# A new instruction order for agent attention with an expert stage: loads batch by batch, TensorE's changes of kind priced by pair

## The chip, the core and the metric

One core of a Trainium2 chip runs the whole program in one launch. The core has five instruction streams, each of which runs in its own order: TensorE (PE in the tables, with its weight loads as PEld), VectorE (DVE), ScalarE (ACT), GpSimd (POOL) and SyncE (SP), which here issues nearly all of the transfers between device memory and the on-chip buffers. The metric is the device time of one execution in microseconds; the median over several executions counts.

## The reference

Four batches of 12608 tokens of 128 channels pass through two softmax products over 49 agents; then 128 tokens of each batch, those with the highest gate score, pass through an expert of two layers.

```python
def sm(a, b):
    s = scale * (a @ b.transpose(0, 2, 1))
    s = s - s.max(-1, keepdims=True)
    e = np.exp(s)
    return e / (e.sum(-1, keepdims=True) + 1e-09)
agent_v = sm(agents, k) @ v
x = sm(q, agents) @ agent_v
# expert stage, batch by batch
top_idx = np.argpartition(-scores[b], capacity)[:capacity]   # scores = x @ w_gate, capacity = 128
h = np.maximum(x[b, top_idx] @ w1, 0.0)
out[b, top_idx] = x[b, top_idx] + sigmoid(scores) * (h @ w2)
```

## The kernel before

**Tiling.** A batch is cut into seven chunks: six of 15 columns of 128 tokens and one of 9. For each batch and chunk there is a load of transposed keys (`xT_b_c` from `kT`), of values (`v_b_c`, one more column of ones) and of transposed queries (`xT_b_c` from `qT`); a large one is 960 KB (0.98 MB), a small one 0.59 MB. All of them, and the output tiles `og` of three batches, share one ring of six buffers (`inp`, N_IN = 6).

**Stages of a batch `b`.** `k`: TensorE makes the scores of a chunk in two halves (`S`, four matmuls side by side in 32-column tiles each), VectorE transposes each half into `sk` and takes its maximum (`mx`). `kmax`: two small products (`mT`, `mB`) make the maximum per agent of all seven chunks and spread it over the partitions (`mb`). `exp`: GpSimd subtracts it from `sk`, ScalarE takes the exponential. `av`: TensorE multiplies `sk` with `v`. `fin`: two small products (`pw`, `pp`) normalise and scale the result into `ws`. `q`: scores of the queries into `sq` (as for keys, with `qm` as maximum). `qe`: GpSimd subtracts, ScalarE takes the exponential; the value is split into two f16 halves in `f` by ScalarE and GpSimd (batch 0 also divides by its sum here). `turn`: TensorE transposes `f` (`fT`), ScalarE or VectorE copies it to `ft`. `gate`: a three-column product per token column gives the gate score (`pg`). `rank`: the 128 best tokens are found (`all`, `gt`, `pc`). `fill` (batch 0) and `out` (the others): TensorE forms the output (`po`), two engines scale it into `og`, SP stores it. `expert`: rows are gathered (`xq`), recomputed, put through the two layers (`ph`, `py`) and scattered (`out` from `ey`), batches 0, 1 and 2 as one group and batch 3 as another. The keys' `sk` tiles have a ring of nine buffers (N_SK = 9), so with seven chunks of one batch alive only two of the next batch find room until the first `av` of the older batch is done.

**What sets the order.** The body records every operation with what it depends on. `place` then runs a list scheduler over them: an operation that is ready is taken by its rank, a number in the table RANKS for its stage, batch, chunk and engine, less a bonus (STICK) if its kind is that of the last one on the engine; on TensorE a change of kind is charged in the planner's time (AFTER, line 253, used at line 352), and SLACK is added for what TensorE hands to others. Every engine's instructions are emitted in the order that comes out, and each engine then waits in that order. The constants are loaded at the top of `agent_attention_moe`: the agents (`ag_sb`), the table of constants (`cst`, 0.29 MB) and the gate weights (`wg_sb`) are issued from ScalarE's queue and their two ends of the expert's weights from SP's.

```python
key = rank[op.seq]
if op.kind == last[e]:
    key = (key[0] - stick, key[1])
...
if last[e] != op.kind:
    op.start += AFTER.get(last[e], 50.0)
```

Of the kernel before, what the change touches and what calls it, by code (L numbers as in the profile page):

```python
# [285 lines left out]
def place(rec, urgency, slack=0.0, stick=0.0):  # L286
# [89 lines left out]
    ('kmax', 0): {"DVE": -294641.053, "PE": -133586.107},  # L376
    ('exp', 0, 0): {"POOL": -143817.163, "ACT": -125982.646},
    ('exp', 0, 1): {"POOL": -963.973, "ACT": -99042.757},
    ('exp', 0, 2): {"POOL": -12481.222, "ACT": -37799.646},
    ('exp', 0, 3): {"POOL": -38853.391, "ACT": -33869.568},  # L380
    ('exp', 0, 4): {"POOL": 16185.168, "ACT": 11872.97},
    ('exp', 0, 5): {"POOL": 28821.359, "ACT": 10861.678},
    ('exp', 0, 6): {"POOL": 14920.899, "ACT": -98349.058},
    ('v', 0, 0): {"SP": -4348.542},
    ('av', 0, 0): {"PE": 5144.545},
    ('v', 0, 1): {"SP": -20520.697},
    ('av', 0, 1): {"PE": 41745.014},
    ('v', 0, 2): {"SP": -3630.195},
    ('av', 0, 2): {"PE": -28204.714},
    ('v', 0, 3): {"SP": -1826.223},  # L390
    ('av', 0, 3): {"PE": -44870.335},
    ('v', 0, 4): {"SP": -689.478},
    ('av', 0, 4): {"PE": -6385.343},
    ('v', 0, 5): {"SP": -461.295},
    ('av', 0, 5): {"PE": 47815.339},
    ('v', 0, 6): {"SP": -404.037},
    ('av', 0, 6): {"PE": 43409.94},
    ('fin', 0): {"DVE": -143642.174, "PE": -132722.281, "POOL": -39179.482, "ACT": -144313.857},
    ('q', 0, 0): {"SP": -704.547, "PE": 9683.405, "DVE": -297487.497},
    ('qe', 0, 0): {"POOL": 11484.086, "ACT": -127061.75, "DVE": -286160.382},  # L400
    ('turn', 0, 0): {"PE": -25559.309, "DVE": -3909.353, "ACT": -76846.925},
    ('gate', 0, 0): {"PE": 21754.42},
    ('q', 0, 1): {"SP": -11511.72, "PE": -165916.237, "DVE": -81122.367},
    ('qe', 0, 1): {"POOL": -9668.74, "ACT": 88899.289, "DVE": 62352.526},
    ('turn', 0, 1): {"PE": -33340.912, "DVE": -134369.208, "ACT": -37052.354},
    ('gate', 0, 1): {"PE": 19893.715},
    ('q', 0, 2): {"SP": -9823.687, "PE": -68234.899, "DVE": 12201.11},
    ('qe', 0, 2): {"POOL": 9370.151, "ACT": 15865.887, "DVE": -114474.214},
    ('turn', 0, 2): {"PE": 25264.138, "DVE": 6840.329, "ACT": -32474.095},
    ('gate', 0, 2): {"PE": 56157.267},  # L410
    ('q', 0, 3): {"SP": -351.313, "PE": 32070.707, "DVE": 29764.455},
    ('qe', 0, 3): {"POOL": 179974.323, "ACT": -58982.455, "DVE": -279699.82},
    ('turn', 0, 3): {"PE": -176895.194, "DVE": -411535.852, "ACT": -99983.463},
    ('gate', 0, 3): {"PE": 5350.803},
    ('q', 0, 4): {"SP": -771.424, "PE": 55087.906, "DVE": 8565.114},
    ('qe', 0, 4): {"POOL": 4649.777, "ACT": 3589.366, "DVE": -115177.183},
    ('turn', 0, 4): {"PE": 38836.4, "DVE": -333689.299, "ACT": -55756.92},
    ('gate', 0, 4): {"PE": 28409.364},
    ('q', 0, 5): {"SP": -27570.937, "PE": -30576.771, "DVE": 39150.54},
    ('qe', 0, 5): {"POOL": 58629.766, "ACT": -105534.475, "DVE": 142558.346},  # L420
    ('turn', 0, 5): {"PE": 25230.881, "DVE": -77845.226, "ACT": 26338.297},
    ('gate', 0, 5): {"PE": 45468.366},
    ('q', 0, 6): {"SP": 34.59, "PE": 22004.194, "DVE": 21572.571},
    ('qe', 0, 6): {"POOL": -284390.957, "ACT": -340814.293, "DVE": -327633.78},
    ('turn', 0, 6): {"PE": 14051.261, "DVE": -303021.527, "ACT": -40022.947},
    ('gate', 0, 6): {"PE": -166324.648},
    ('rank', 0): {"DVE": -507.176, "PE": 9903.499, "ACT": 9822.614},
# [7 lines left out]
    ('kmax', 1): {"DVE": -2570.807, "PE": 11129.379},  # L435
    ('exp', 1, 0): {"POOL": -99995.468, "ACT": -36076.047},
    ('exp', 1, 1): {"POOL": -12644.966, "ACT": -75342.068},
    ('exp', 1, 2): {"POOL": -22999.565, "ACT": -273703.34},
    ('exp', 1, 3): {"POOL": -11794.752, "ACT": 50941.528},
    ('exp', 1, 4): {"POOL": 12391.852, "ACT": -70255.562},  # L440
    ('exp', 1, 5): {"POOL": -8726.541, "ACT": -265905.419},
    ('exp', 1, 6): {"POOL": -45627.909, "ACT": -159584.905},
    ('v', 1, 0): {"SP": -1531.14},
# [1059 lines left out]
```

## Time and profile before

| | us |
|---|---|
| median of 3 runs | 304.13 (303.07 to 308.46) |
| the profiled execution, its own time | 303.28 |
| its span in the profile | 301.5 |
| TensorE busy | 269.3 |
| VectorE busy | 221.3 |
| GpSimd busy | 186.4 |
| ScalarE busy | 169.7 |

The span is what the profile covers; 1.78 us of the execution's own time lie outside it. An engine is busy while one of its computing instructions runs; several of TensorE's overlap, so its busy time is the time in which at least one runs. In the views "idle before" is the time that the engine stood still ahead of an instruction, with what ended the wait. All computing instructions are recorded by the scheduler and issued from one line (L1424 before, L1435 after), so they are told apart by the names of their tiles.

### The profile page before, as it was taken

What the parts mean: (1) busy time and instruction counts of PE and PEld (TensorE: products, weight loads), DVE (VectorE), ACT (ScalarE), POOL (GpSimd) and SP (SyncE); (2) the same over time, 40 slices, a digit from 0 to 9 for tenths busy, and PEclk for the clock granted to TensorE, in tenths of its full rate; (3) what the DMA queues carried; (4) which work ended last, traced back from release to release, by engine and by line L of the source; (5) the groups of instructions that cost most, each with busy time, mean ns of one, the idle gap of its engine ahead of it and who ended that gap; (6) DMA issues with size and microseconds to landing.
All of it is one profiled execution on the core that took longest, in us unless ns stands there. A gap on an engine that the chain in (4) does not pass through costs nothing. (4 is left out here: it accounts for less than half of the span.)

```text
span 301.5 us, 8552 instructions
## 1 busy us (share of the span) xinstructions
PE 269.3 (89%) x3524; PEld 177.9 (59%) x3524; DVE 221.3 (73%) x507; ACT 169.7 (56%) x306; POOL 186.4 (62%) x158
## 2 busy tenths in 40 slices
PE   1986897899998999998999999999699999999990
PEld 0232333474555674455555743775688999898890
DVE  2788899867796549975799669889338869996530
ACT  1284354557834857640389415499599847954510
POOL 7372656999762995640299333799642764895241
PEclk9999999999999999999999999999999989999997
DMA  7999999999998999999999999687885299989950
GB/s 279 419 417 414 424 414 410 389 424 421 417 421 349 343 374 421 412 380 384 424 417 376 420 419 366 240 316 231 302 281 190 114 382 374 391 341 410 422 202 24
DMA packets 18203, 106.68 MB, mean 354 GB/s; under 512 B 2032, under 2 KB 3440, under 8 KB 18160
## 3 DMA queue, kind: packets, MB, share of 16 engines
q1 hardware_dynamic: 17472, 105.07, 87.8%
q8 instruction: 30, 0.49, 0.7%
q0 software_dynamic: 256, 0.52, 0.6%
q10 hardware_dynamic: 432, 0.48, 0.5%
q14 instruction: 13, 0.11, 0.1%
HBM read 79.85 MB, written 26.21 MB: 352 GB/s over the span
## 5 line engine op out<-in xcount | busy, mean ns | idle before, releaser
L1424 PE MATMUL S<-xT,ag_sb 128*32 128x480 f32 (+1 forms) x896 | 100.7, 561 | 17.4 <-DMA ag_sb<-agT 6.2
L1424 PEld LDWEIGHTS <-ft 128*128 128x128 f16 x1188 | 59.6, 99 | 21.2 <-issue 18.3
L1424 POOL TENSOR_TENSOR sq<-sq,qm 128x735 f32<-128x735 f32 (+1 forms) x35 | 47.8, 1368 | 39.1 <-DVE qm L1424 39.1
L1424 POOL TENSOR_TENSOR f<-sq,f 128x735 f16<-128x735 f32 (+1 forms) x28 | 42.8, 1531 | 34.6 <-ACT f L1424 24.7
L1424 PEld LDWEIGHTS S<-xT,ag_sb 128*32 128x32 f32 x896 | 24.2, 110 | 58.5 <-issue 23.8
L1424 PE MATMUL po<-ws,ft 128*128 128x128 f16 x792 | 55.7, 223 | 2.0 <-ACT og L1424 0.9
L1424 ACT COPY ft<-fT 128x896 f16<-128x896 f16 (+2 forms) x49 | 43.3, 896 | 20.0 <-PE fT L1424 11.2
L1424 PE MATMUL av<-v,sk 128*64 128x129 f32 x792 | 51.2, 276 | 2.3 <-issue 1.9
L1424 POOL TENSOR_TENSOR sk<-sk,mb 128x735 f32<-128x735 f32 (+1 forms) x28 | 46.9, 1707 | 6.0 <-DVE mb L1424 6.0
L1424 PEld LDWEIGHTS av<-v,sk 128*64 128x64 f32 x792 | 44.2, 136 | 10.2 <-issue 5.3
L1424 POOL TENSOR_TENSOR og<-og,r 128x512 f32<-128x512 f32 (+1 forms) x39 | 36.3, 944 | 16.8 <-ACT og L1424 15.8
L1424 DVE STREAM_TRANSPOSE sq<-S 128x480 f32<-128x480 f32 (+1 forms) x56 | 35.3, 641 | 10.5 <-PE S L1424 9.9
L1424 DVE STREAM_TRANSPOSE sk<-S 128x480 f32<-128x480 f32 (+1 forms) x56 | 34.8, 636 | 7.1 <-PE S L1424 4.9
L1424 DVE TENSOR_REDUCE mx<-S 128x1 f32<-128x480 f32 (+1 forms) x56 | 33.1, 610 | 7.1 <-PE S L1424 6.8
L1424 ACT ACTIVATE sq<-sq,lift 128x735 f32<-128x735 f32 (+1 forms) x28 | 24.8, 886 | 17.8 <-POOL sq L1424 17.8
L1424 PEld LDWEIGHTS <-f 128*128 128x128 f16 x396 | 23.6, 98 | 18.2 <-issue 10.0
L1424 PE MATMUL fT<-idh,f 128*128 128x128 f16 x396 | 29.7, 219 | 2.5 <-POOL f L1424 1.1
L1424 ACT CAST f<-sq 128x735 f16<-128x735 f32 (+1 forms) x28 | 22.2, 791 | 16.6 <-PE fT L1424 10.1
L1424 DVE TENSOR_REDUCE qm<-sq 128x15 f32<-128x735 f32 (+1 forms) x35 | 30.0, 861 | 1.9 <-ACT sq L1424 1.3
L1424 DVE TENSOR_TENSOR og<-po,r 128x512 f32<-128x512 f32 (+1 forms) x42 | 26.7, 655 | 3.2 <-PE av L1424 1.2
L1424 ACT ACTIVATE sk<-sk 128x735 f32<-128x735 f32 (+1 forms) x28 | 22.1, 793 | 10.8 <-POOL sk L1424 10.6
L1424 DVE SCALAR_TENSOR_TENSOR gt<-all,top,minus 128x512 bf16<-128x512 f32 x32 | 23.7, 740 | 2.6 <-PE all L1424 2.1
(131 smaller groups left out, 236.3 us busy)
## 6 DMA issues: line engine op xcount, KB each, us to landing
v<-va SPq DMA_DIRECT2D x24, 967.5 KB, 8.1
xT<-qT SPq DMA_DIRECT2D x24, 960.0 KB, 8.7
xT<-kT SPq DMA_DIRECT2D x24, 960.0 KB, 7.8
out<-og SPq DMA_DIRECT2D x24, 960.0 KB, 6.2
v<-va SPq DMA_DIRECT2D x4, 580.5 KB, 9.3
xT<-kT SPq DMA_DIRECT2D x4, 576.0 KB, 6.3
xT<-qT SPq DMA_DIRECT2D x4, 576.0 KB, 9.1
out<-og SPq DMA_DIRECT2D x4, 576.0 KB, 9.7
```

The lines of the kernel that those rows point to most:

```text
L1424: call(*args, **kwargs)
```

## The change

The planner's numbers change in four places: SLACK becomes 0, STICK is halved, the charge for a change of kind on TensorE depends on the pair of kinds, and the whole table RANKS is new. The loads of `cst` and `wg_sb` move from ScalarE's queue to SP's and get ranks of their own. No operation is added or removed, no size and no buffer count changes.

```diff
-SLACK = 18.436502753594528
-STICK = 13170.561655066054
+SLACK = 0.0
+STICK = 6130.565386853517
...
-AFTER = {"S": 90.0, "av": 200.0, "po": 100.0, "fT": 20.0}
+HALF = ("po", "fT", "pg")
...
+def switch(a, b):
+
+    if a in HALF and b in HALF:
+        return 10.0
+    return 160.0 if a == "av" else 100.0 if a == "S" or b in ("S", "av") else 50.0
...
-                    op.start += AFTER.get(last[e], 50.0)
+                    op.start += switch(last[e], op.kind) if last[e] else 50.0
...
-    ('k', 0, 0): {"SP": -28164.939, "PE": 35409.862, "DVE": -82619.513},
...
+    ('k', 0, 0): {"SP": -558242.88, "PE": -60419.549, "DVE": -307691.923},
...
-    nc.scalar.dma_start(cst, consts)
+    with rec.at("const", 0):
+        nc.sync.dma_start(cst, consts)
...
-    nc.scalar.dma_start(wg_sb, wgb)
+    with rec.at("const", 1):
+        nc.sync.dma_start(wg_sb, wgb)
```

SP's queue, at the start of the program. In a name such as `xT_1_2_312` the first number is the batch, the second the chunk, the last a running number; `qT`, `kT` and `va` tell queries, keys and values apart. Before:

```order
L1424 DMA xT_1_2_312<-qT 128x1920
L1424 DMA xT_2_2_443<-qT 128x1920
L1424 DMA xT_1_0_293<-qT 128x1920
L1424 DMA xT_0_3_125<-kT 128x1920
L1424 DMA xT_0_0_113<-kT 128x1920
L1424 DMA xT_0_5_209<-qT 128x1920
L1424 DMA w1_end_94<-w1 128x128
L1424 DMA w2_end_95<-w2 128x128
L1424 DMA xT_0_1_117<-kT 128x1920
L1424 DMA xT_0_5_133<-kT 128x1920
L1424 DMA v_0_1_148<-va 128x1935
L1424 DMA xT_2_4_461<-qT 128x1920
```

The same place in the changed kernel:

```order
L1435 DMA xT_0_0_113<-kT 128x1920
L1435 DMA xT_0_6_137<-kT 128x1152
L1435 DMA v_0_0_146<-va 128x1935
L1435 DMA xT_0_3_125<-kT 128x1920
L1435 DMA xT_0_0_163<-qT 128x1920
L1435 DMA xT_0_4_129<-kT 128x1920
L1435 DMA w1_end_94<-w1 128x128
L1435 DMA w2_end_95<-w2 128x128
L1435 DMA wg_sb_93<-wgb 128x128
L1435 DMA cst_92<-consts 128x562
L1435 DMA xT_0_2_121<-kT 128x1920
L1435 DMA xT_0_5_133<-kT 128x1920
```

Queries of batches 1 and 2 have left the start; the keys of batch 0 stand there, with one tile of values and one of queries of the same batch, and the two constants come after six loads. The last key of batch 0 is SP's entry 13 now and was its entry 18; the last value of batch 0 is entry 30 and was 37.

TensorE, around the first `av` of batch 0. Before, it was the 239th row of TensorE's list:

```order
L1424 MATMUL av_0_147<-v_0_0_146,sk_0_0_112 64x129 x15
L1424 MATMUL S_1_4_0_260<-xT_1_4_259,ag_sb_91 32x480 x4
L1424 MATMUL S_1_4_1_261<-xT_1_4_259,ag_sb_91 32x480 x4
L1424 MATMUL S_1_3_0_256<-xT_1_3_255,ag_sb_91 32x480 x4
L1424 MATMUL S_1_3_1_257<-xT_1_3_255,ag_sb_91 32x480 x4
L1424 MATMUL av_0_147<-v_0_1_148,sk_0_1_116 64x129 x10
```

Now it is the 59th:

```order
L1435 MATMUL S_1_1_0_248<-xT_1_1_247,ag_sb_91 32x480 x4
L1435 MATMUL S_1_1_1_249<-xT_1_1_247,ag_sb_91 32x480 x4
L1435 MATMUL S_1_2_0_252<-xT_1_2_251,ag_sb_91 32x480 x4
L1435 MATMUL S_1_2_1_253<-xT_1_2_251,ag_sb_91 32x480 x4
L1435 MATMUL av_0_147<-v_0_0_146,sk_0_0_112 64x129 x15
L1435 MATMUL av_0_147<-v_0_1_148,sk_0_1_116 64x129 x15
L1435 MATMUL S_1_5_0_264<-xT_1_5_263,ag_sb_91 32x480 x4
L1435 MATMUL S_1_5_1_265<-xT_1_5_263,ag_sb_91 32x480 x4
```

The first `av` of the program has moved up past most of the query work that stood ahead of it; the third key chunk of batch 1 (`S_1_2`), whose `sk` tile is the tenth of the ring of nine, stands just ahead of it.

Over the whole list of TensorE the runs of one kind are 246 before and 242 now (`S` 51 and 56, `po` 53 and 50, `fT` 45 and 38, `av` 28 and 23, `pg` 14 and 20); the longest unbroken runs of `pg` were 99, 75 and 60 and are 75, 45 and 45.

## Rows read from the trace of the kernel before

**Rows 1.** The page: the span, and the DMA rate in 40 equal slices.
```profile
span 301.5 us, 8552 instructions
...
GB/s 279 419 417 414 424 414 410 389 424 421 417 421 349 343 374 421 412 380 384 424 417 376 420 419 366 240 316 231 302 281 190 114 382 374 391 341 410 422 202 24
```

**Rows 2.** Busy time by stretch (engine, instructions), granted clock, DMA share, GB/s.
```profile
0.00:60.00 60.00, 44.77 (x452) 17.39 (x452) 47.13 (x89) 27.62 (x39) 37.36 (x38) 1.00 0.98 396
60.00:226.00 166.00, 157.54 (x2141) 99.04 (x2142) 123.59 (x276) 100.90 (x173) 107.64 (x77) 1.00 0.95 370
226.00:295.00 69.00, 67.00 (x933) 61.49 (x931) 50.20 (x142) 41.22 (x96) 40.46 (x44) 0.98 0.77 310
295.00:301.50 6.50, 0.00 (x0) 0.00 (x0) 0.35 (x1) 0.00 (x0) 0.97 (x1) 0.70 0.08 25
...
0.00:15.00 15.00, 8.25 (x58) 2.01 (x62) 7.23 (x17) 3.29 (x7) 8.14 (x18) 1.00 0.89 348
```

**Rows 3.** What TensorE waited for: total us, times, longest.
```profile
PE S L1424 <- DMA ag_sb<-agT: 6.2, 1, 6.2
PE S L1424 <- DVE sk L1424: 3.7, 2, 2.1
...
PE av L1424 <- issue: 1.9, 1, 1.9
```

**Rows 4.** Timeline of TensorE: start us, us, operation, count.
```profile
63.11 1.01 PE L1424 MATMUL S<-xT,ag_sb 128*32 128x480 f32 x8
64.05 4.18 PE L1424 MATMUL av<-v,sk 128*64 128x129 f32 x70
68.16 1.01 PE L1424 MATMUL fT<-idh,f 128*128 128x128 f16 x15
...
72.98 1.82 PE L1424 MATMUL S<-xT,ag_sb 128*32 128x480 f32 x16
74.73 0.62 PE L1424 MATMUL fT<-idh,f 128*128 128x128 f16 x8
```

**Rows 5.** Stretch of 2 us, columns as in rows 2.
```profile
248.00:250.00 2.00, 2.00 (x21) 2.00 (x20) 1.79 (x8) 0.95 (x3) 0.60 (x1) 0.54 1.05 436
```

**Rows 6.** Timeline of TensorE around the stretch of rows 5.
```profile
237.94 1.85 PE L1424 MATMUL po<-ws,ft 128*128 128x128 f16 x30
...
243.98 2.78 PE L1424 MATMUL pg<-ws,ft 128*128 128x3 f16 x99
246.62 3.35 PE L1424 MATMUL po<-ws,ft 128*128 128x128 f16 x30
```

**Rows 7.** Timeline of all engines, from batch 0's kmax to its first av.
```profile
49.00 0.27 PE L1424 MATMUL mT<-idf,m 128*2 128x128 f32 x1
...
52.69 3.53 POOL L1424 TENSOR_TENSOR sk<-sk,mb 128x735 f32<-128x735 f32 x2 [2.40 <-DVE mb L1424]
...
55.40 0.87 PE L1424 MATMUL av<-v,sk 128*64 128x129 f32 x11
```

**Rows 8.** The page's costliest groups: busy us, mean ns of one, idle before.
```profile
L1424 POOL TENSOR_TENSOR sq<-sq,qm 128x735 f32<-128x735 f32 (+1 forms) x35 | 47.8, 1368 | 39.1 <-DVE qm L1424 39.1
L1424 POOL TENSOR_TENSOR f<-sq,f 128x735 f16<-128x735 f32 (+1 forms) x28 | 42.8, 1531 | 34.6 <-ACT f L1424 24.7
...
L1424 POOL TENSOR_TENSOR sk<-sk,mb 128x735 f32<-128x735 f32 (+1 forms) x28 | 46.9, 1707 | 6.0 <-DVE mb L1424 6.0
...
L1424 ACT ACTIVATE sq<-sq,lift 128x735 f32<-128x735 f32 (+1 forms) x28 | 24.8, 886 | 17.8 <-POOL sq L1424 17.8
...
L1424 ACT CAST f<-sq 128x735 f16<-128x735 f32 (+1 forms) x28 | 22.2, 791 | 16.6 <-PE fT L1424 10.1
```

**Rows 9.** The page's DMA issues: KB each, us from issue to landing.
```profile
xT<-qT SPq DMA_DIRECT2D x24, 960.0 KB, 8.7
```

**Rows 10.** Timeline of all engines: the table of constants has landed.
```profile
9.33 0.47 ACT L1424 CAST x<-cst 128x1 bf16<-128x1 f32 x4 [5.90 <-DMA cst<-consts]
```

**Rows 11.** DMA rate from 226 to 295 us, in 40 slices of 1.725 us.
```profile
GB/s 377 375 102 7 0 0 9 142 423 423 279 406 408 425 427 419 396 178 423 375 419 365 112 427 427 406 396 423 428 391 400 415 416 427 427 223 419 183 45 50
```

More of the change, by code (lines that the diff above doesn't have):

```diff
@@ L367 @@
 RANKS = {
-    ('setup', 0): {"ACT": -112998.916, "POOL": -41330.235, "DVE": -60677.881},
[7 rows of a table removed]
[L376 to L427, printed above, removed]
[7 rows of a table removed]
@@ L435 @@
[L435 to L443, printed above, removed]
@@ L632 @@
-    ('out', 2, 26): {"PE": 8451.522, "DVE": -1587.638, "ACT": 19515.271, "POOL": 90020.124, "SP": 4214.483},
-    ('out', 2, 27): {"PE": 14860.73, "DVE": -11166.581, "ACT": 37748.738, "POOL": 22703.145, "SP": -15127.125},
-    ('expert', 2): {"POOL": 37647.797, "PE": 179474.28, "DVE": -120776.12, "ACT": -228756.011},
-    ('expert', 3): {"POOL": 22951.733, "PE": 74238.18, "DVE": -138033.187, "ACT": 84384.947},
+    ('setup', 0): {"ACT": -123995.537, "POOL": -226775.386, "DVE": -330989.174},
[9 rows of a table added]
+    ('kmax', 0): {"DVE": -300206.643, "PE": -380208.421},
@@ new lines @@
+    ('gate', 0, 5): {"PE": -1672.094},
+    ('q', 0, 6): {"SP": 32459.619, "PE": -78358.108, "DVE": -345672.163},
+    ('qe', 0, 6): {"POOL": -27991.134, "ACT": 1439150.817, "DVE": -278880.289},
+    ('turn', 0, 6): {"PE": -17005.632, "DVE": -633966.746, "ACT": -777417.642},
+    ('gate', 0, 6): {"PE": 26270.986},
+    ('rank', 0): {"DVE": -446766.326, "PE": -172242.925, "ACT": -262911.069},
[7 rows of a table added]
+    ('kmax', 1): {"DVE": -350079.182, "PE": -425310.542},
+    ('exp', 1, 0): {"POOL": -118014.402, "ACT": 1098377.658},
@@ new lines @@
+    ('turn', 1, 2): {"PE": -355624.568, "ACT": 955330.754},
+    ('gate', 1, 2): {"PE": 620462.051},
+    ('q', 1, 3): {"SP": 41757.771, "PE": 30839.917, "DVE": -227921.899},
+    ('qe', 1, 3): {"POOL": 68257.906, "ACT": 1850475.73},
+    ('turn', 1, 3): {"PE": -16908.022, "ACT": 12395.229},
+    ('gate', 1, 3): {"PE": 32935.564},
+    ('q', 1, 4): {"SP": 42525.767, "PE": -487662.049, "DVE": 73745.809},
+    ('qe', 1, 4): {"POOL": 582884.166, "ACT": 886960.248},
+    ('turn', 1, 4): {"PE": 8157.362, "ACT": 401148.205},
@@ new lines @@
+    ('gate', 1, 4): {"PE": -179875.682},
+    ('q', 1, 5): {"SP": 43756.473, "PE": 18263.577, "DVE": 112204.08},
+    ('qe', 1, 5): {"POOL": 19270.315, "ACT": 1762395.711},
+    ('turn', 1, 5): {"PE": 31038.115, "ACT": 1850548.195},
+    ('gate', 1, 5): {"PE": 63331.63},
+    ('q', 1, 6): {"SP": 50286.516, "PE": -349161.909, "DVE": -12804.369},
+    ('qe', 1, 6): {"POOL": -68284.931, "ACT": 1442992.742},
+    ('turn', 1, 6): {"PE": 49015.397, "ACT": 978312.709},
+    ('gate', 1, 6): {"PE": -547496.865},
@@ new lines @@
+    ('exp', 2, 6): {"POOL": 7257.048, "ACT": -777835.629},
+    ('v', 2, 0): {"SP": 50661.319},
+    ('av', 2, 0): {"PE": -189090.389},
+    ('v', 2, 1): {"SP": 52855.88},
+    ('av', 2, 1): {"PE": 23961.053},
+    ('v', 2, 2): {"SP": 53977.159},
+    ('av', 2, 2): {"PE": 5800.695},
+    ('v', 2, 3): {"SP": 48097.88},
+    ('av', 2, 3): {"PE": -216136.664},
+    ('v', 2, 4): {"SP": 57847.117},
+    ('av', 2, 4): {"PE": 129721.977},
+    ('v', 2, 5): {"SP": 54483.257},
+    ('av', 2, 5): {"PE": -13097.003},
@@ new lines @@
+    ('gate', 2, 3): {"PE": 61060.05},
+    ('q', 2, 4): {"SP": 71307.055, "PE": -45898.819, "DVE": -50474.118},
+    ('qe', 2, 4): {"POOL": -322983.588, "ACT": 2295760.202},
+    ('turn', 2, 4): {"PE": -43503.09, "ACT": 1986757.411},
+    ('gate', 2, 4): {"PE": -68162.924},
+    ('q', 2, 5): {"SP": 77318.706, "PE": -628023.259, "DVE": 11561.519},
+    ('qe', 2, 5): {"POOL": -42392.193, "ACT": 1627195.79},
+    ('turn', 2, 5): {"PE": -39576.307, "ACT": 1017309.433},
+    ('gate', 2, 5): {"PE": 54969.386},
@@ new lines @@
+    ('q', 2, 6): {"SP": 78259.749, "PE": -378400.619, "DVE": -214022.535},
+    ('qe', 2, 6): {"POOL": 633480.489, "ACT": 1668811.458},
+    ('turn', 2, 6): {"PE": 45756.628, "ACT": 2352812.325},
+    ('gate', 2, 6): {"PE": 60699.887},
+    ('rank', 2): {"DVE": -282034.834, "ACT": 1150380.206, "PE": -135799.619},
[7 rows of a table added]
+    ('kmax', 3): {"DVE": -322202.419, "PE": -478446.931},
+    ('exp', 3, 0): {"POOL": -315673.344, "ACT": 332372.515},
+    ('exp', 3, 1): {"POOL": 216280.263, "ACT": -474059.325},
+    ('exp', 3, 2): {"POOL": 93055.81, "ACT": 630302.37},
@@ new lines @@
+    ('gate', 3, 2): {"PE": 48638.999},
+    ('q', 3, 3): {"SP": 139105.002, "PE": -85153.335, "DVE": -227504.136},
+    ('qe', 3, 3): {"POOL": 566663.921, "ACT": 1314853.353},
+    ('turn', 3, 3): {"PE": 114774.796, "ACT": -1533357.49},
+    ('gate', 3, 3): {"PE": -545249.947},
+    ('q', 3, 4): {"SP": 96519.304, "PE": 88294.059, "DVE": -46927.805},
+    ('qe', 3, 4): {"POOL": -315745.809, "ACT": 1919440.847},
+    ('turn', 3, 4): {"PE": 101543.597, "ACT": 1322390.143},
+    ('gate', 3, 4): {"PE": -41878.466},
```

346 lines of the change are left out of this document (172 added, 174 removed), and 56 rows, old and new, of the table RANKS.

## The prediction

> **What bounds the kernel now.** I read the page's span and DMA rate first [rows 1], then the busy times by stretch [rows 2], then what TensorE waits for [rows 3]. The reader should see two bounds that take turns. Until about 60 us the loads set the pace: the DMA rate is near 415 GB/s from the second slice on [rows 1], 23.8 MB have come in by 60 us (396 GB/s times 60), and TensorE is busy for 44.77 of the 60 us. From 60 to 295 us TensorE itself is the bound: busy 157.54 of 166 and 67.00 of 69 us, so idle for only 8.46 and 2.0 us [rows 2]. Then 6.5 us follow in which the last expert rows are added and scattered. So the span is TensorE's busy time of 269.3 plus 15.2 us of idle time up to 60 us (6.2 of them the wait for the agents [rows 3]), 10.5 between 60 and 295, and 6.5 at the end. VectorE, 47.13 of 60 us busy in the first stretch, is close behind there: TensorE waits 3.7 us for its `sk` transposes, two waits up to 2.1 us long [rows 3].
>
> No operation is added or removed, so the change can gain only out of these three idle parts, out of the cost of changing kind, and out of the clock.
>
> **The start, until 60 us.** I count what the first 23.8 MB contain in each order. Before, that is SP's entries 1 to 26, now 1 to 28: 17 large and 2 small score tiles, 5 queries among them, and 5 value tiles. TensorE's price for one: two halves of scores 1.75 us (72.98 to 74.73), a small pair 1.2 (an estimate: 288 columns of 480, and the entry of a run), a query's transposes about 0.95, and an `av` of 15 columns, which is 30 matmuls, 1.76 (4.11 us between the starts for 70) [rows 4]. That makes 17 x 1.75 + 2 x 1.2 + 4 x 0.95 + 5 x 1.76 = 44.8 us if everything that has landed is also done. The last three to land (one `av`, two score tiles) are 4.7 us of that and may still be open, so 40 to 44.8 us stand against 44.77 done before. The reason is plain in the order: keys bring 1.75 us of TensorE work per 0.98 MB and the early value tile brings none until kmax, where the queries of other batches brought 2.7. So the start costs time: **+2 us**, ends 0 and +4 (all of the 4.7 open, less what the first stretch lost to VectorE before and may not lose again).
>
> **The middle, 60 to 295 us.** Here the new order has more room. The chain from a query chunk's last score to its first `fT` is VectorE's transposes and maximum, then GpSimd 1.37, ScalarE 0.89 and 0.79, GpSimd 1.53 us [rows 8]: 4.6 us behind VectorE's part, without any queue. Summing TensorE's work between the two places in its list at the prices above, four query chunks of the old order stand within 6 us of their scores (4.8 the closest), none of the new within 8. A load of queries takes 8.7 us from issue to landing [rows 9]; the TensorE work between the release of an input buffer and the first use of what is loaded into it next is under 8.6 us for 12 loads of the old order after the 26th, and for 3 of the new. I take 4.5 of the 10.5 us as gone, **-4.5**. The ends: 8 us gained if nearly all such waits go, and 4 lost if the new order hides waits of its own that the count doesn't see (a chain through GpSimd, an eviction).
>
> **The clock.** From 248 to 250 us the granted clock is 0.54 [rows 5], that is mostly the lower level of 1.2 GHz, right behind a run of 99 three-column `pg` matmuls; the 30 `po` behind it take 3.35 us where 30 others take 1.85 [rows 6]. The longest run is 75 now, and a run of 75 lies in the middle stretch of the old order too, which stands at 1.00 [rows 2]. So **-1.5 us**, ends -1.5 (the dip goes) and +1.5 (it comes at another place).
>
> **Changes of kind.** A run of `S` of one tile's half costs 0.94 us (63.11 to 64.05), two halves in one run 1.75, so entering a run costs about 0.13 us [rows 4]. The runs fall from 246 to 242: **-0.5 us**. What speaks against the change is that the runs of `S` rise from 51 to 56, which alone is +0.7; these are the ends. The Trainium skill, TensorEngine Tiling (Array Packing), Key Properties, says that TensorE drains when the tiling mode changes, not when only the tile does; `S` runs in 32-column and `av` in 64-column tiles, the rest in full ones. By that rule only the changes of mode count, 144 before and 141 now, and the term would be -0.4; the trace's step of 0.13 at entering `S` agrees with a small drain.
>
> **The constants.** ScalarE no longer issues two transfers; SP issues them behind six loads. The table landed by 9.33 us [rows 10]. At SP's place it goes out once the small key tile has landed, near 7 us, behind about 4 MB in flight (10 us at 415 GB/s), so it lands near 17 us. ScalarE's first work behind its casts is the exponential of the query tile that is SP's entry 5, whose chain reaches ScalarE near 19 us, and VectorE's two users stand behind the fifth score tile. So 0, covered by that wait; up to +1 if the cover fails.
>
> **The end.** The outputs of 22 chunks go out behind the last loads, at about 415 GB/s from 240 to 288 us, after a gap of nearly 10 us without transfers [rows 11]. In the new order 23 remain, but the first of them complete some 6 us of TensorE work earlier in the list, and 10 us of expert matmuls still follow the last `po` (8 before). So 0, ends 0 and +3. The 6.5 us behind the last matmul stay.
>
> **The sum.** 301.5 + 2 - 4.5 - 1.5 - 0.5 = 297.0 us of span. The profiled execution took 1.78 us outside its span, which gives 298.8 against its own 303.28, -1.5%; the median of the runs was 304.13, 0.28% above, which gives 299.6.
>
> **Rivals.** *The order runs almost without waits*: the middle keeps 2.5 of 10.5 us, the start loses nothing. 301.5 - 8 - 1.5 - 0.5 = 291.5, as a median 294. For it speaks that every distance I counted grew; against it, that 23.8 MB of the new order hold less work.
>
> *The change does not do what it says*: pairs are priced, yet only four runs fewer come out, and the waits of the middle turn up at other places. Then -0.5 from the kinds against +2 at the start: 303, as a median 305.6. For it: an order fitted to a planner's clock meets other durations on the chip, as the old one did, which still has 10.5 us of waits.
>
> *The ring of nine holds the start* (the slower side). VectorE's transpose of the third key tile of batch 1 needs the buffer of batch 0's first `sk`, so it waits in VectorE's order until the first `av` is done, and all of VectorE's work behind it with it. Batch 0's last key is the 13th load, 9.1 MB in: 15 us at 348 GB/s and 3.9 MB at 416, so 24.3 us. Scores and maxima take some 2.7 us more. From `mT` to the first `av` it was 6.4 us [rows 7], and GpSimd now does another chunk's subtraction of 1.7 first [rows 8], so the first `av` can begin at 35 us. TensorE is ready for it when the loads up to entry 18 (14.0 MB, 36.1 us) are through, near 37.5. The margin is 2 us. Behind it GpSimd has seven `sk`, four `sq` and two `f` steps, 20.5 us, from 31 to 51.5 us, where TensorE asks for the last of them at 52 us. If both margins fail by 4 us each, +8 joins the start's +2 and the rest stays out: 311.5 of span, 314 as a median. It decides from about 6 us of delay on. Against it: the old order met the same ring with the same chain and lost no more than a few tenths there.
>
> *The outputs queue up at the end*: +3 at the end and half of the middle's gain: 302.3, as a median 305.
>
> **Chances.** Forecast 0.42 (own range 295 to 304), nearly without waits 0.20, waits only moved 0.15, outputs 0.06, ring 0.17 (any delay there of 6 us or more). A measurement of this kernel can tell some 2% from no change, that is below 298.0 or above 310.2. Faster: the 0.20 and a third of the forecast, 0.34. Slower: the ring, 0.17. Within: 0.49. The range from 292 to 311 leaves out part of the ring's case and the rim of the stall-free one, under 0.2.
>
> **What will show it.** Right at the start if TensorE's busy time by 60 us is 41 to 45 us and the first `av` begins between 35 and 39 us; the ring's case shows in VectorE waiting for `av` there. Right in the middle if TensorE's idle time from 60 us to its last matmul is 4 to 8 us, with fewer waits of `fT` and `av`; wrong if it is above 10. The clock: no stretch near 0.5 behind a `pg` run. The kinds: busy time within 1 us of 269.3 less the clock's part. The end: outputs at some 415 GB/s without a gap, and 6.5 us behind the last matmul. If the span falls by more than 8 us, I have missed a gain, most likely at the start.

## The result, and the profile after

| | before | after |
|---|---|---|
| median of 4 runs, us | 304.22 (303.07 to 308.46) | 294.31 (293.69 to 296.67) |
| ratio to before | | 0.970 (0.963 to 0.978) |
| the profiled execution, its own time | 303.28 | 294.86 |
| span in the profile | 301.5 | 293.0 |
| TensorE busy | 269.3 | 265.7 |
| TensorE idle up to 60 us | 15.2 | 14.7 |
| idle from 60 us to its last matmul | 10.0 | 4.2 |
| from its last matmul to the end | 7.0 | 8.4 |

The changed kernel is faster, by 3.0% (2.2 to 3.7). The last four lines make up the span, and so the gain: 8.5 us of span are 3.6 of busy time, 0.5 at the start and 5.8 of idle time behind it, less 1.4 lost at the end.

Busy time by stretch in the changed kernel, columns as in [rows 2]:

```profile
0.00:60.00 60.00, 45.26 (x478) 20.70 (x482) 46.01 (x88) 17.55 (x27) 33.49 (x34) 1.00 0.98 401
60.00:226.00 166.00, 162.47 (x2229) 102.51 (x2221) 129.55 (x311) 117.47 (x201) 111.28 (x79) 1.00 0.93 371
226.00:284.60 58.60, 57.93 (x829) 53.29 (x826) 42.61 (x108) 34.93 (x80) 38.50 (x43) 1.00 0.87 352
284.60:293.00 8.40, 0.00 (x0) 0.00 (x0) 0.35 (x1) 0.00 (x0) 2.92 (x3) 0.63 0.13 39
```

The first row is nearly that of before: 45.26 us busy against 44.77, at 401 GB/s against 396. The second has lost most of its idle time, 3.53 us against 8.46. The granted clock is 1.00 until the last matmul; the slice at 0.54 of [rows 5] has no successor.

What TensorE waited for between 60 us and its last matmul, columns as in [rows 3], all rows of the view:

```profile
PE S L1435 <- DMA xT<-qT: 1.6, 3, 0.8
PE S L1435 <- DMA xT<-kT: 0.9, 2, 0.5
PE po L1435 <- ACT og L1435: 0.6, 2, 0.4
PE po L1435 <- ACT gt L1435: 0.5, 1, 0.5
PE fT L1435 <- ACT ft L1435: 0.4, 2, 0.2
PE po L1435 <- DVE og L1435: 0.3, 1, 0.3
```

2.5 of these 4.3 us are loads. The wait of `av` of 1.9 us in [rows 3] is gone; the view names no releaser for it, and by its place it was probably a load too (a tile of batch 3's values, issued late). The same view of before adds up to 9.7 us. Its rows of `fT`:

```profile
PE fT L1424 <- POOL f L1424: 1.1, 3, 0.5
PE fT L1424 <- ACT ft L1424: 0.7, 2, 0.5
PE fT L1424 <- DVE iv L1424: 0.5, 1, 0.5
```

The waits of `fT` went from 2.3 to 0.4 us, those of small products and scores for VectorE (`mT`, `pc`, two of `S`) from 1.5 to nothing, those of `po` for `og` from 1.4 to 0.9.

### The profile page after: what moved, and what is told of

Read it like the earlier page. It is cut to its first block, busy times and chain, and to the rows that moved or that the text cites. A ratio compares the mean times of both kernels' runs of the same rounds, so it can differ in the third digit from the quotient of the medians.

```text
span 293.0 us, 8554 instructions
## 1 busy us (share of the span) xinstructions
PE 265.7 (91%) x3524; PEld 176.5 (60%) x3524; DVE 218.5 (75%) x507; ACT 169.9 (58%) x306; POOL 186.2 (64%) x158
## 4 chain that ended last, share of the span: by engine, by line
PE 44%; ACT 7%; DMA 7%; DVE 2%; issue 2%; POOL 1%; POOLq 0%; DVEq 0%
PE po L1435 13%; PE S L1435 8%; PE av L1435 8%; DMA xT<-qT 7%; PE fT L1435 4%; PE ph L1435 3%; ACT gt L1435 2%; PE all L1435 2%; PE pg L1435 2%; PE py L1435 2%; ACT ft L1435 2%; ACT sq L1435 1%; POOL out L1435 1%; ACT f L1435 1%; DVE og L1435 1%
## 5 line engine op out<-in xcount | busy, mean ns | idle before, releaser
L1435 PE MATMUL S<-xT,ag_sb 128*32 128x480 f32 (+1 forms) x896 | 101.3, 560 | 16.3 <-DMA ag_sb<-agT 6.2
L1435 PEld LDWEIGHTS <-ft 128*128 128x128 f16 x1188 | 58.1, 97 | 18.3 <-issue 16.3
L1435 ACT COPY ft<-fT 128x896 f16<-128x896 f16 (+2 forms) x49 | 43.4, 900 | 20.3 <-PE fT L1435 20.2
L1435 PE MATMUL po<-ws,ft 128*128 128x128 f16 x792 | 53.2, 219 | 1.6 <-ACT og L1435 0.6
L1435 PE MATMUL av<-v,sk 128*64 128x129 f32 x792 | 50.5, 276 | 0.4 <-DMA v<-va 0.4
L1435 DVE STREAM_TRANSPOSE sq<-S 128x480 f32<-128x480 f32 (+1 forms) x56 | 35.7, 645 | 14.5 <-PE S L1435 11.5
L1435 DVE STREAM_TRANSPOSE sk<-S 128x480 f32<-128x480 f32 (+1 forms) x56 | 35.6, 639 | 9.3 <-PE S L1435 7.0
L1435 PEld LDWEIGHTS <-f 128*128 128x128 f16 x396 | 22.9, 98 | 13.6 <-issue 8.9
L1435 PE MATMUL fT<-idh,f 128*128 128x128 f16 x396 | 28.7, 220 | 0.5 <-ACT ft L1435 0.4
L1435 ACT COPY og<-po 128x512 f32<-128x512 f32 (+1 forms) x39 | 20.7, 538 | 9.4 <-PE po L1435 7.1
```

The costliest lines, as they stand in the source:

```text
L1435: call(*args, **kwargs)
```

## The experiments

In the runs called frozen the planner is left out: the operations are emitted by a list of numbers, which is the order of before or of the changed kernel, with the named operations moved by hand:

```diff
-    order = place(rec, urgency, SLACK, STICK)
+    order = [rec.ops[i] for i in ORDER]
```

The account of all runs, made as in the first table (page, first 60 us, last `py` matmul), with the medians of the timed runs and the ratio to before on the same chip:

| run | median us | ratio (95%) | span | busy | idle to 60 | idle to last matmul | end |
|---|---|---|---|---|---|---|---|
| before | 304.2 | | 301.5 | 269.3 | 15.2 | 10.0 | 7.0 |
| after | 294.3 | 0.970 (0.963 to 0.978) | 293.0 | 265.7 | 14.7 | 4.2 | 8.4 |
| e1 | 309.8 | 1.013 (1.007 to 1.019) | 308.1 | 271.7 | 15.1 | 15.0 | 6.4 |
| e2 | 294.0 | 0.961 (0.955 to 0.967) | 295.0 | 267.4 | 14.8 | 4.9 | 7.9 |
| e3 | 314.8 | 1.030 (1.023 to 1.036) | 315.3 | 274.9 | 14.5 | 20.2 | 5.7 |
| e4 | 306.4 | 1.003 (0.999 to 1.006) | 305.7 | 272.0 | 14.8 | 11.9 | 7.0 |
| e5 | 308.5 | 1.019 (1.010 to 1.027) | 306.4 | 281.4 | 15.0 | 2.1 | 7.9 |
| e6 | 296.4 | 0.979 (0.970 to 0.987) | 294.3 | 267.0 | 14.0 | 5.3 | 8.0 |
| e7 | 303.6 | 0.999 (0.993 to 1.005) | 298.9 | 268.9 | 15.7 | 7.9 | 6.4 |
| e8 | 295.0 | 0.974 (0.963 to 0.986) | 293.4 | 265.1 | 15.3 | 4.4 | 8.6 |
| e9 | 320.2 | 1.052 (1.045 to 1.059) | 319.5 | 281.2 | 12.7 | 18.0 | 7.6 |
| e10 | 333.3 | 1.097 (1.090 to 1.104) | 330.7 | 280.2 | 14.1 | 28.9 | 7.6 |
| e11 | 295.8 | 0.974 (0.967 to 0.981) | 294.4 | 267.5 | 14.3 | 4.8 | 7.8 |
| e12 | 314.5 | 1.034 (1.028 to 1.041) | 313.3 | 273.3 | 13.9 | 17.9 | 8.2 |

One profiled execution stands for a median only within some 3 us (that of e2 took 296.9 us, that of e7 300.75): e7 differs from before in one small move at 244 us, and yet its span is 2.6 us shorter and its loads cost less waiting, while its median is that of before. The clock differs from one execution to the next too: its mean over an execution is 0.985 to 0.996 in the four of the changed kernel, and 0.966 to 0.998 in those of before that were timed beside the experiments.

### Which part of the change carries it: e1, e9, e10, e2

**e1: the new table, the old planner rules.**

```diff
-SLACK = 0.0
-STICK = 6130.565386853517
+SLACK = 18.436502753594528
+STICK = 13170.561655066054
...
-                    op.start += switch(last[e], op.kind) if last[e] else 50.0
+                    op.start += AFTER.get(last[e], 50.0)
```

> The new table placed by the old planner rules (the flat price per kind left, 18.4 ns of slack, the old bonus for staying with a kind). The order this gives has the same first 59 entries on SP, 236 runs of one kind against 242, and no query chunk with less than 7.6 us of TensorE work between its last score and its first fT (7.8 to 8.8 in the changed kernel, 5.8 before, all by the same prices). Theory A, the table's distances carry the gain: a span of 292 to 296 us and 3.5 to 5.5 us of TensorE idle time between 60 us and its last matmul. Theory B, the pair prices carry it: 297 to 302 us, with most of the waits of the middle back (8 us or more).

The span is 308.1 us, beyond both expectations and the time 1.3% above before, although both counts that the prediction went by are better in it than in the order of before: no chunk below 7.6 us of distance, six late loads (12 before, 3 after). Up to 60 us it equals the changed kernel; the loss lies behind. Where TensorE waited from 60 us on (the three largest rows):

```profile
PE S L1428 <- DVE sq L1428: 3.5, 5, 1.0
PE po L1428 <- DVE og L1428: 2.5, 3, 0.9
PE po L1428 <- ACT og L1428: 2.1, 5, 0.8
```

8.1 of 14.6 us are waits for a PSUM bank (a part of the buffer that TensorE writes to) that VectorE or ScalarE has not yet emptied; the changed kernel has 0.9 us of that kind (`po` for `og`). Neither count sees such a wait. Against the changed kernel the span is 15.1 us longer: 7.2 are these waits, 3.6 others, and 6.0 are busy time, part of it where the clock fell (below); 2.0 came back at the end.

**e9: one number of the planner set back, 18.4 ns of slack.**

```diff
-SLACK = 0.0
+SLACK = 18.436502753594528
```

> The changed kernel with one number of the planner set back: 18.4 ns of slack instead of none; the table, the pair prices, the bonus and the constants stay. The order comes out otherwise all the same, 262 runs of one kind against 258 counted with the expert's. Theory A, the pair prices carry the gain: the prices are kept, so the span is 292 to 295 us. Theory B, the table is a list of settings for one planner clock and any change of that clock makes another order: 298 to 309 us with 8 to 15 us of TensorE idle time between 60 us and the last matmul, most of it where S and po wait for VectorE's and ScalarE's evictions.

**e10: the flat prices, all else new.**

```diff
-                    op.start += switch(last[e], op.kind) if last[e] else 50.0
+                    op.start += AFTER.get(last[e], 50.0)
```

> The changed kernel with the flat prices of before instead of the pair prices; slack and bonus are the new ones, as are the table and the constants. Theory A, pair prices carry the gain: 300 to 309 us. Theory B, the table fits one planner clock: the same range, so this run tells something only beside the run with the slack alone. Theory C, the bonus for staying (halved by the change) carries it, since longer runs of S and po meet three and four PSUM banks: 293 to 297 us.

320.2 and 333.3 us. With the pair prices in place, 18 ns of planner time cost 26 us of device time, so the prices alone don't carry the gain, and neither does the halved bonus, which e10 keeps. That is theory B, only stronger than I had put it. The largest waits of e9 from 60 us on:

```profile
PE fT L1435 <- POOL f L1435: 3.6, 3, 1.9
PE po L1435 <- ACT og L1435: 3.4, 4, 1.6
PE S L1435 <- DVE sq L1435: 2.7, 6, 0.8
PE po L1435 <- DVE og L1435: 1.7, 2, 0.9
```

Waits are only a part of the loss. TensorE was busy for 15.5 us longer than in the changed kernel in e9 and 14.5 in e10: in slices of 2 us the granted clock fell to 0.50 in five stretches of e9 and four of e10, and nowhere ahead of the last matmul in the changed kernel.

The table is thus a setting for one planner clock, found together with it; what came to the chip is one order among many that the same table gives for slightly other clocks, and this one is good. The opposite half, the old table under one of the new rules (the slack, the bonus or the prices), has no order at all: the planner comes to a state in which no instruction can begin. The gain can't be shared out between table and rules.

**e2: the constants back on ScalarE's queue**, the rest of the changed order frozen.

```diff
-    with rec.at("const", 0):
-        nc.sync.dma_start(cst, consts)
+    nc.scalar.dma_start(cst, consts)
```

> The changed kernel's order, frozen, with the two loads of constants back on ScalarE's queue at the start. If the constants' place is worth nothing, as forecast (0 to +1): the span within 1 us of the changed kernel's 293.0, TensorE busy for 44.5 to 46 us by 60 us. If the move itself bought the start (-0.5 instead of +2): the first 60 us lose 1 to 2.5 us of busy time and the span is 294 to 295.5.

45.2 us busy by 60 us, as in the changed kernel, and the same median: the place of the constants is worth nothing that these runs can tell. The span of 295.0 is 2 us longer for another reason: TensorE waited 0.6 us longer for a load of queries at 193 us, and behind this stretch (busy for 1.63 of the 4 us from 190) the clock stood at 0.72 and 0.50 in the next two slices of 2 us.

### Does distance take the waits: e4

The order of before, frozen; the `turn` operations of seven chunks, with their copies, moved back by 1 to 4 us of TensorE work. For batch 1, chunk 6, with 4 us of other work between the two places:

```diff
-fT(1,6) of columns 0 to 7, its copy to ft, fT(1,6) of column 8, its copy
...
+fT(1,6) of columns 0 to 7, its copy to ft, fT(1,6) of column 8, its copy
```

> The order of before, frozen, with the transposes fT of the seven chunks that stand closest behind their scores (5.8 to 8.9 us of TensorE work) moved back by 1 to 4 us of work; the smallest distance becomes 6.6, the next 8.0 us. Nothing else moves; runs of one kind rise by six. Theory, distance takes the waits: the 2.0 us of waits of fT behind 60 us fall below 0.8, the six runs cost 0.5 to 0.8, the span is 0.5 to 1.5 us shorter, 300 to 301. Rival, the waits move on to the users behind: fT's waits fall but the idle time of the middle stays within 0.5 us of 10.5, and the span is 301.5 to 302.5.

The waits of `fT` fell from 2.3 us to 0.7, and all idle time rose, to 11.9 us against 10.0. The three largest waits from 60 us on:

```profile
PE S L1229 <- DMA xT<-kT: 2.7, 4, 1.1
PE av L1229 <- issue: 1.8, 1, 1.8
PE S L1229 <- DVE sq L1229: 1.4, 1, 1.4
```

The wait of 1.4 us for `sq` is new. Why it and the longer waits for loads came isn't shown: e7, in nearly the order of before, has 0.2 us for keys where before has 1.2, so such rows also differ from one execution to the next. The ratio of the medians is 1.003 (0.999 to 1.006), which leaves out the 0.5 to 1.5 us that distance was to bring. The rival of this run stands: distance alone doesn't shorten the time.

### The price of a change of kind: e5, e6

Both frozen in the changed order, with operations of two kinds laced at 18 places each (`A B` becomes half of A, half of B, the rest of A, the rest of B), where no wait was in sight. e5 laces S with full-tile kinds, e6 full-tile kinds with each other.

```diff
-    ... A, B, ...
+    ... (A, 0, h), (B, 0, k), (A, h, None), (B, k, None), ...
```

> The same lacing at 18 places where fT, po and pg meet each other: 36 more entries, none of them a change between S or av and a full tile (141 such changes, as in the changed kernel). If every entry costs 0.13 us: busy time +4.7 us, as in the run that laces S. If only changes between S or av and full tiles cost (the new prices: 10 ns within this group, 50 to 160 elsewhere): busy time within 0.6 us of 265.7, the span 293 to 294.

Busy time rose by 1.4 us, 0.04 for an entry, and not by 4.7. Even that is too much: up to the same matmul in both traces, 0.9 of the 1.4 us lie outside the 18 places, and e8, which adds no entry, is 0.6 us off the changed kernel too. The price is better read at a place itself. One of them in the changed kernel, from the start of `po` to the start of `pg`:

```profile
135.89 0.62 PE L1435 MATMUL po<-ws,ft 128*128 128x128 f16 x8
...
136.85 0.54 PE L1435 MATMUL pg<-ws,ft 128*128 128x3 f16 x15
```

and in e6, with two entries more:

```profile
135.65 0.40 PE L1243 MATMUL po<-ws,ft 128*128 128x128 f16 x4
135.88 0.39 PE L1243 MATMUL fT<-idh,f 128*128 128x128 f16 x4
136.10 0.39 PE L1243 MATMUL po<-ws,ft 128*128 128x128 f16 x4
...
136.61 0.54 PE L1243 MATMUL pg<-ws,ft 128*128 128x3 f16 x15
```

Both take 0.96 us. So it is at ten of the 18 places, within 0.005 us; the other eight add 0.5 us together. An entry among these kinds costs nothing.

Sums over the page's groups mislead here: those of `po`, `fT` and `pg` rise by 5.5 us from the changed kernel to e6 (56.1 for 53.2, 30.0 for 28.7, 14.8 for 13.5), 0.15 per entry. At a change the first matmul of the new run is already counted while the last of the old one still is: above, `po` starts at 135.65 and lasts 0.40 us, and `fT` starts at 135.88.

> The changed kernel's order, frozen, with 18 places between 85 and 225 us at which a run of S meets one of fT, po or pg laced: half of the one, half of the other, and again. That is 36 more entries into a run, all of them changes between S and a full tile; no work is added. If every entry costs the 0.13 us that the trace of before gave for S: TensorE's busy time rises from 265.7 by 4.7 us. If only the 18 entries into S cost: by 2.3 us. If entries cost nothing: within 1 us of 265.7. The span follows the busy time, 297 to 298, 295 to 296, or 293 to 294.

Busy time rose by 15.7 us, more than any expectation, and S has all of it (117.0 us against 101.3 in the groups). Most of that isn't the entries. A place in the changed kernel (between the two lines stand eight `po`):

```profile
95.41 1.82 PE L1435 MATMUL S<-xT,ag_sb 128*32 128x480 f32 x16
...
97.62 1.11 PE L1435 MATMUL all<-idf,top 128*128 128x128 f32 x8
```

and in e5 (four `po` stand on either side of the half group):

```profile
96.07 1.80 PE L1242 MATMUL S<-xT,ag_sb 128*32 128x480 f32 x12
...
98.14 1.00 PE L1242 MATMUL S<-xT,ag_sb 128*32 128x480 f32 x4
...
99.30 0.89 PE L1242 MATMUL all<-idf,top 128*128 128x128 f32 x6
```

The four products of an S group run side by side in 32-column tiles, so half of a group (x4) takes 1.00 us, as a whole one does (x8, 1.01 in [rows 4]), and a group that is cut in two costs twice. Within a run the half group adds 0.79 us (1.80 less 1.01). The place takes 3.23 us instead of 2.21, so 0.23 us remain for two more changes between S and a full tile. At the ten places that stand alone the two changes and the half group add 0.86 to 1.07 us, about 1.0 at most of them. A change of the tiling mode (the tile width in which TensorE works) thus costs about 0.1 us each here, an estimate from these starts, where a change between kinds in full tiles costs nothing. The run's total can't show this: 0.81 us for each of 18 groups is 14.6 of the 15.7 us, and two of the groups are of the small tile and cheaper.

### The clock: e7, e11

**e7: the order of before, frozen, one `po` of eight put into the run of 99 `pg`.** On TensorE's list:

```diff
 pg(3,0), pg(3,2), pg(3,1), pg(3,4)
+po(1,3) of columns 4 to 7
 pg(3,6), pg(3,5), pg(3,3)
...
-po(1,3) of columns 4 to 7
```

> The order of before, frozen, with one po of eight matmuls (batch 1, chunk 3, and its eviction) moved into the run of 99 pg at 244 us, which becomes runs of 60 and 39. If the run of 99 is what the clock falls behind: no slice from 246 to 250 us below 0.9, the 30 po behind it take about 1.85 us instead of 3.35, and busy time falls by 1.5 us, the span to 300 (or to 300.5 to 301 where a wait for the batch's ranking takes a part of it). If the dip has another cause: it stays near 0.54 and the span at 301.5.

```profile
241.50 1.74 PE L1229 MATMUL pg<-ws,ft 128*128 128x3 f16 x60
243.10 0.61 PE L1229 MATMUL po<-ws,ft 128*128 128x128 f16 x8
243.55 1.18 PE L1229 MATMUL pg<-ws,ft 128*128 128x3 f16 x39
244.59 3.36 PE L1229 MATMUL po<-ws,ft 128*128 128x128 f16 x30
```

The 30 `po` behind it still take 3.36 us, and the slices from 244 to 248 us stand at 0.65 and 0.50. The run being unbroken is not the point.

**e11: the changed order, frozen, batch 3's seven gates joined into one run of 99.**

```diff
-pg(3,0), pg(3,1), pg(3,2)
...
-pg(3,5)
...
-pg(3,3)
...
-pg(3,4)
...
+pg(3,0), pg(3,1), pg(3,2), pg(3,5), pg(3,3), pg(3,4)
 pg(3,6)
```

> The changed kernel's order, frozen, with the seven gates of batch 3 joined into one run of 99 pg at the place of the last one (236.77 us); before they stood as 45, 15, 15, 15 and 9 between 227 and 237 us. If such a run is what the clock falls behind: a slice of 2 us at 0.5 to 0.7 within 4 us behind it, TensorE's busy time up by 1 to 1.5 us, the span 294 to 294.5. If not: no slice under 0.9 from 230 to 260 us, the span 292.5 to 293.5.

```profile
238.00:240.00 2.00, 2.00 (x36) 1.88 (x33) 1.54 (x6) 1.22 (x5) 0.67 (x1) 0.72 1.03 419
240.00:242.00 2.00, 2.00 (x16) 1.91 (x15) 1.39 (x7) 0.98 (x5) 1.20 (x2) 0.50 0.79 323
```

Behind the run (235.60 to 238.38 us) the clock falls as expected, TensorE's busy time rises by 1.8 us, the span by 1.4. (The medians, 295.8 and 294.3 us, are too close to tell apart.) The dip also came behind the 99 of e4, in nearly the order of before. But it didn't in e3, where the same 99 stand in nearly that order too and the clock is 1.00 from 250 to 268 us:

```profile
260.13 2.78 PE L1229 MATMUL pg<-ws,ft 128*128 128x3 f16 x99 [0.27 <-POOL ws L1229]
262.77 1.85 PE L1229 MATMUL po<-ws,ft 128*128 128x128 f16 x30
```

So a run of 99 can bring the dip and does not always; what decides is open. In the profiled executions there was none behind 75 in a row (at 78 us in the changed kernel), nor behind 75 and 24 with eight `po` and a wait between (at 211 us before). e1 adds a case: its planner put 84 in a row, the clock fell while `po` ran right behind them, and from 256 to 264 us it stood at 0.50:

```profile
251.62 2.38 PE L1428 MATMUL pg<-ws,ft 128*128 128x3 f16 x84
...
259.11 3.12 PE L1428 MATMUL all<-idf,top 128*128 128x128 f32 x13 [1.29 <-DVE top L1428]
```

### More buffers, and the end: e3, e12, e8

**e3 and e12: seven buffers for loads, one for early outputs**, e3 in the order of before (18 `po` matmuls of one early chunk moved so that two early outputs are never filled at a time), e12 in the changed order together with the edit of e8.

```diff
-N_IN = 6
+N_IN = 7
...
-N_OG = 2
+N_OG = 1
```

> The order of before, frozen, with seven buffers for loads instead of six; the second staging buffer of the early outputs pays for the room, for which 18 po matmuls move. Loads can start one buffer earlier. Theory: TensorE's waits on loads behind 60 us (1.18 and 0.39 us at 140 to 144 us, 1.88 at 217.85, some 0.9 in small ones, 4.4 in all) come from a buffer that is released too late; then 3 to 4.5 us go, a span of 297 to 298.5. Rival: they only move to other waits, a span of 300.5 to 302.

> The changed kernel's order, frozen, with seven buffers for loads and one staging buffer for early outputs (in this order no two of them are filled at a time), and with the split expert outputs, batch 3's scatter now ahead of batch 2's, which waits for its last output to land. Theory: the 2.5 us of waits on loads behind 60 us fall below 1, and three scatters are done before batch 2's output lands: 1.5 us from the middle and 0.5 to 1 us at the end, a span of 290.5 to 291.5. Rival: the one staging buffer holds TensorE up as in the run with the order of before (waits of po for ScalarE's og of more than 1 us): 295 us or more.

They are slower by about 10 and 20 us than the orders that they come from, and the waits lead to the buffer that paid for the seventh. e12 from 60 us on:

```profile
PE po L1240 <- ACT og L1240: 9.8, 5, 3.5
PE pg L1240 <- ACT ft L1240: 5.4, 1, 5.4
PE S L1240 <- DMA xT<-kT: 1.3, 2, 0.8
```

In e3 the first of these rows is 11.5 us. A staging tile is free only when its transfer has landed, 3.2 to 7.9 us behind its issue for the outputs before 250 us in e12; ScalarE waits for that, and TensorE behind ScalarE. ScalarE's wait in e12, from 150 to 250 us:

```profile
ACT og L1240 <- DMA out<-og: 16.4, 5, 5.5
```

The clock adds to it: behind these waits it fell to 0.50 in three stretches of e12, which was busy for 7.6 us longer than the changed kernel. Loads made TensorE wait less (1.3 us against 2.5 in the changed order), but with TensorE so far behind this doesn't show what a seventh buffer alone would be worth. As a test of the load waits e3 decides nothing.

**e8: one PSUM bank for each expert output of batches 0 to 2**, the changed order frozen, each addition and scatter right behind its product.

```diff
-        py = pm("py", C)
+        py = [
+            pool.tile([P, 512], F32, tag=ring, name=f"py{g}_{tag}")[:, :C] for g in range(G)
+        ]
```

> The changed kernel's order, frozen, with one PSUM bank for each of the three expert outputs of batches 0 to 2 instead of one for all; each is added and scattered as soon as its own product is there, and batch 2's scatter stands ahead of batch 3's. In the changed kernel four scatters of 0.97 to 1.04 us, 0.3 us apart, run one behind the other from 283.47 us, and the last starts at 287.37, 2.8 us behind the last matmul. If GpSimd's queue of scatters sets the end: the last one starts about 0.7 us behind the last matmul and the time from the last matmul to the end falls from 8.4 to 6.3 us, the span to 291. If the scatters' landing sets it: 8 us or more remain and the span stays at 293.

In the changed kernel the four scatters stand in a row. Timeline, last product and scatters:

```profile
283.47 1.04 POOL L1435 DMA_INDIRECT out<-ey,idx  x1 [7.44 <-DVE ey L1435]
...
284.20 0.39 PE L1435 MATMUL py<-w_end,hT 128*128 128x128 f32 x2
284.81 0.98 POOL L1435 DMA_INDIRECT out<-ey,idx  x1 [0.30 <-issue]
...
287.37 0.97 POOL L1435 DMA_INDIRECT out<-ey,idx  x1 [0.30 <-issue]
```

e8 takes that row apart, and another wait is right behind it:

```profile
281.02 0.98 POOL L1240 DMA_INDIRECT out<-ey,idx  x1 [2.25 <-DVE ey L1240]
...
287.50 0.97 POOL L1240 DMA_INDIRECT out<-ey,idx  x1 [5.50 <-DMA out<-og]
288.77 0.97 POOL L1240 DMA_INDIRECT out<-ey,idx  x1 [0.30 <-issue]
```

Batch 2's rows may be scattered only when its last output has landed, at 287.5 us in e8, 0.1 us behind the start of the last scatter before the edit. In e12, where batch 3's scatter goes first, the last one starts 3.1 us behind the last matmul for the same reason. So two bounds lie close together at the end: GpSimd's scatters in the changed kernel, and right behind them the outputs' transfers (398 to 418 GB/s there from 242 to 278 us). No run was measurably faster than the changed kernel; e2's median of 294.0 us is that of the changed kernel.

## Why the prediction was right or wrong

The forecast was 299.6 us, the time 294.3: inside the range of 292 to 311, just outside the 295 to 304 that I had given 0.42, on the side that I had given 0.34. Term by term the working forecast -4.5 us of span, and -8.5 came; the 4 us between are 2.5 at the start, 1.3 in the middle and 1.6 of busy time too little, less 1.4 at the end. The last sign that I had named came true: the span fell by more than 8 us, and the largest part that I missed is at the start.

**The start** (forecast +2, came -0.5). TensorE was busy for 45.26 us by 60 us, just above my 41 to 45. The step that failed is the comparison: I set the new order's work, priced from rows, against the old order's measured 44.77 us. By 60 us, shape by shape, before:

```profile
L1424 PE MATMUL S<-xT,ag_sb 128*32 128x480 f32 x272 | 33.1, 608 | 14.8 <-DMA ag_sb<-agT 6.2 <-DVE sk L1424 3.7 <-DMA xT<-kT 2.3
L1424 PE MATMUL fT<-idh,f 128*128 128x128 f16 x99 | 7.3, 220 | 0.0
L1424 PE MATMUL S<-xT,ag_sb 128*32 128x288 f32 x48 | 3.9, 410 | 0.0
```

and in the changed kernel:

```profile
L1435 PE MATMUL S<-xT,ag_sb 128*32 128x480 f32 x264 | 31.6, 588 | 14.3 <-DMA ag_sb<-agT 6.2 <-DMA xT<-kT 4.2 <-DMA xT<-qT 1.9
L1435 PE MATMUL av<-v,sk 128*64 128x129 f32 x150 | 9.4, 275 | 0.4 <-DMA v<-va 0.4
```

A tile of scores is 16 passes, a chunk's transposes 15, an `av` 30. The changed kernel had done 16.5 large tiles and one small (16 passes), three chunks of transposes (45) and five `av`: 41.7 us at my prices. Before, it was 17 large, three small, 6.6 chunks of transposes and one `av` (30): 41.4 us at the same prices. Priced alike the two orders differ by 0.3 us, measured by 0.5; my prices were about 3.5 us too low for either. About 3 us of the 44.8 were still undone, so that part of the reasoning held. The loads set the same pace in both (401 and 396 GB/s), and they bring as much work in the one order as in the other: that the early value tile brings nothing until kmax is true, but it brings its work before 60 us all the same.

**The ring of nine** did not hold the start. The first `av` began at 39.74 us, later than my 35 to 39; VectorE waited for it for 0.49 us, at 41.83 us, and its `sk` cost TensorE 0.5 us instead of 3.7.

**The middle** (forecast -4.5, came -5.8; the other runs in the changed order, e2, e6, e8 and e11, have 4.4 to 5.3 us of idle time there, so on average it is nearer to -5). The size was about right, and half of the reason. The waits of `fT`, which I had named, fell from 2.3 us (2.0 in e7, nearly the order of before) to 0.4, and stay at 0.2 to 0.4 in e2, e6, e8 and e11. For the loads, which I had named too, nothing is shown: 2.5 us now and 4.1 before (with the 1.9 of `av`), but 2.2 in e7. The waits of small products and scores for VectorE (1.5 us before, 1.7 in e7, none now) I had not counted.

The two counts by which I chose these waits don't foretell an order: they put e1 between before and the changed kernel, and the chip puts it behind both; e4 improves the first count and gains nothing. (Counted again for e1 and e4, the closest chunk came out at 5.8 us before and 7.8 in the changed kernel, where the prediction has 4.8 and no less than 8.) What they leave out is the third thing that TensorE waits for, PSUM banks that VectorE and ScalarE empty: 8.1 us in e1, 7.8 in e9, 15.2 in e10 (4.9 and 3.3 of `po` for `og`, 3.7 and 3.3 of `S` and `po` for `sq`). Before has only 1.4 and the changed kernel 0.9 (`po` for `og`), so these waits tell what other orders lose, and hardly what this one gained. Why this order keeps them small is open, since no run changed that alone.

**The clock** (forecast -1.5). The dip is gone. It is worth 1.5 us by the 30 `po` of before ([rows 6]) and 1.8 by the busy time of e11, where it returned. The step "right behind a run of 99" needs two corrections: 60 and 39 with 0.45 us of `po` between bring it as well, and the same 99 don't in e3. Since the clock differs between executions of one kernel, that the whole term came as forecast is in part luck.

**Changes of kind** (forecast -0.5). The places in e5 and e6 give nothing for a change among full tiles and about 0.1 us for one of the mode. There are three of the latter less, 0.3 us. The step of 0.13 us that I read for a run of `S` fits that; what was wrong was to charge it to every run. The Trainium skill, TensorEngine Tiling (Array Packing), Key Properties, says that TensorE drains when the tiling mode changes and not when only the tile does. The traces agree, with 0.23 us for two changes of mode in e5 and 0.00 for two without one in e6. Of the 3.6 us by which busy time fell, 1.5 to 1.8 are the clock's and 0.3 these; some 1.5 to 1.8 us have no owner in my account.

**The constants** (forecast 0, up to +1) are 0 as far as e2 can tell.

**The end** (forecast 0, ends 0 and +3) came to +1.4. The last product of batches 0 to 2 and that of batch 3 now end 1.8 us apart (282.8 and 284.6), where 4.3 us lay between them before, so four scatters, 1.3 us from start to start, stand in a row. I had not counted GpSimd's side of the last 7 us.

**The rivals.** The time is that of the order that runs almost without waits (294, to which I had given 0.20): the start lost nothing, as there, but the middle kept 4.2 us instead of 2.5 and the end lost 1.4, and that the lower busy time made up for them is luck. "The change does not do what it says" was half right in its reason: pair prices alone are not what gains (e9 has them and takes 320 us), and an order does meet other durations on the chip than in the planner. That is why a table must be judged by its order on the chip and not by the rules behind it.

## What to carry to other kernels

An order that a planner made from a fitted table is one object: changing a planner's constant by 18 ns under it gave 26 us, and neither of the two counts tried here foretold it; time the order itself, and freeze it before changing anything near it. Count for every engine that feeds or empties TensorE, PSUM banks too: in the three worse orders they held TensorE for 8 to 15 us. Compare a priced sum with a sum at the same prices, and not with a measured time. The price of an event is read at its place, from start to start against the same place in the other run: sums over groups count overlapping instructions twice, and a whole run's busy time carries what differs elsewhere.

## What the runs showed of the hardware

Four 32-column products run side by side: half of such a group took 1.00 us, the whole 1.01. A change between these and full tiles cost about 0.1 us (0.23 for two in e5), a change of operation within full tiles nothing (0.96 us with and without two more in e6). The granted clock fell to 0.50 behind 84 (e1) and 99 (e11) three-column matmuls although TensorE was busy all the time, though not behind the 99 of e3, and it fell behind waits (e2: busy 1.63 of 4 us, then 0.72 and 0.50), so that a late load costs more than its wait (e2 has 0.7 us more of idle time than the changed kernel, and 1.7 us more of busy time). A scatter of 128 rows holds GpSimd for 0.97 to 1.04 us, and the next one follows 0.3 us later.
